# Seven block products for eight in the up-projection of the last 3072 tokens

## Chip, cores and metric

One core of a Trainium2 chip runs the whole program. The metric is the device time of one execution in microseconds (us). Engines are called as in the profile: PE (TensorE matmul), PEld (its weight loads), DVE (VectorE), ACT (ScalarE), POOL (GpSimd), SP (the queue that issues the DMAs).

## Reference

Attention over 8 batches, 8 heads, 576 positions and 64 channels, with a local mask in the first four heads and a strided one in the others; its output, as 4608 tokens by 512 channels, goes through a feed-forward layer.

```python
mask_local = (rel >= 0) & (rel < stride)                       # stride = 32
mask_strided = (rel >= 0) & (pos[None, :] % stride == pos[:, None] % stride)
...
attn = attn / (np.sum(attn, axis=-1, keepdims=True) + 1e-09)
attn_out = np.matmul(attn, v)
...
x = np.ascontiguousarray(attn_out.transpose(0, 2, 1, 3)).reshape(B * S, H * D)
h = np.maximum(x @ w_in, 0.0)                                  # 512 -> 2048
return (h * h @ w_out).astype(np.float32)                      # 2048 -> 512
```

## The kernel before

Tokens go in 12 chunks of 384 (`TC`). Every operand of the two big products is kept as a high and a low part of type fp32r, and a product is three matmuls: high by high, high by low, low by high.

**Feed-forward.** `up(c, j)` makes one of 16 tiles of 128 hidden units of chunk c: 4 slices of 128 channels by 3 parts, 12 matmuls of 384 columns (L440), in one of three PSUM banks. ACT takes relu and square of it in place (L451, L452) and casts the high part (L453); DVE subtracts to get the low part (L454). `down(c, j)` multiplies that tile into three output tiles: 3 times 3 matmuls of 512 columns (L473). PE takes two `up`, then the two `down` of the tiles before, so that ACT and DVE have the length of two `up` and two `down` for a tile. Chunk after chunk goes on without a break in this pattern.

**Attention** for a chunk is made while PE works on the chunk before it. `pair(c, pr)` does two local heads: 8 score matmuls (L219; the two heads sit in partitions 0 to 63 and 64 to 127, and alternate), masked minima on DVE (L222), 8 exps on ACT (L229), the division on ACT and POOL (L235, L237), 12 small transposes on DVE (L243), 8 output matmuls (L253). `strided(c)` does the other four heads on POOL and DVE alone: products on POOL (L390, L412), each summed by a DVE reduction (L391, L413). `plan` and `SPREAD` say at which tile of a chunk each step is issued. The weights are read once, split by ACT, DVE and POOL during the first chunk, and stay in SBUF.

**Order.** The scheduler fixes one order per engine ahead of time, and each engine keeps to it: an instruction whose data is late holds up all behind it on its engine.

## Time and profile before

| | before |
|---|---|
| median of 3 runs | 887.97 us (887.94 to 888.25) |
| the profiled execution: time | 888.65 us |
| the profiled execution: span | 886.9 us |
| PE busy | 877.0 us, 99% |
| DVE, ACT, POOL busy | 557.0, 444.0, 530.1 us |
| HBM read, written | 52.69 MB, 9.44 MB |

The span is from the first to the last instruction; 1.75 us lie around it. In the timeline a matmul's length holds its way through the array too, so lengths overlap: the time that a matmul takes from PE is the distance from its start to the next one's start.

### The profile page before, as it was taken

What the parts mean: (1) busy time and instruction counts of PE and PEld (TensorE: products, weight loads), DVE (VectorE), ACT (ScalarE), POOL (GpSimd) and SP (SyncE); (2) the same over time, 40 slices, a digit from 0 to 9 for tenths busy, and PEclk for the clock granted to TensorE, in tenths of its full rate; (3) what the DMA queues carried; (4) which work ended last, traced back from release to release, by engine and by line L of the source; (5) the groups of instructions that cost most, each with busy time, mean ns of one, the idle gap of its engine ahead of it and who ended that gap; (6) DMA issues with size and microseconds to landing.
All of it is one profiled execution on the core that took longest, in us unless ns stands there. A gap on an engine that the chain in (4) does not pass through costs nothing.

```text
span 886.9 us, 14492 instructions
## 1 busy us (share of the span) xinstructions
PE 877.0 (99%) x5107; PEld 783.0 (88%) x5107; DVE 557.0 (63%) x1640; ACT 444.0 (50%) x1166; POOL 530.1 (60%) x568
## 2 busy tenths in 40 slices
PE   8999999999999999999999999999999999999997
PEld 7788898989898988898889898989898889898996
DVE  5786677687677677777867868868777333241111
ACT  5999645355355353453544535435535445353332
POOL 3699666767857787887787788788878101000000
PEclk9999999999999999999999999999999999999999
DMA  9852511140031121120211212202101100000000
GB/s 361 334 210 94 186 57 52 62 143 25 18 131 32 66 100 31 57 78 17 76 46 49 64 39 67 64 13 82 58 13 55 31 13 35 14 1 2 35 1 36
DMA packets 21033, 63.06 MB, mean 71 GB/s; under 512 B 2336, under 2 KB 2976, under 8 KB 19424
## 3 DMA queue, kind: packets, MB, share of 16 engines
q1 hardware_dynamic: 20672, 61.81, 20.4%
q8 instruction: 40, 0.66, 0.3%
q10 hardware_dynamic: 288, 0.33, 0.1%
q14 instruction: 33, 0.27, 0.1%
HBM read 52.69 MB, written 9.44 MB: 70 GB/s over the span
## 4 chain that ended last, share of the span: by engine, by line
PE 95%; ACT 2%; POOL 1%; issue 0%; DVE 0%; DVEq 0%; POOLq 0%; ACTq 0%
PE h L440 45%; PE y L473 45%; PE s L219 2%; PE o L253 2%; ACT b L317 1%; PE w_ps L570 1%; PE b L289 1%; POOL w L171 1%; ACT raw L152 0%; ACT z L164 0%; POOL pq L390 0%; ACT w L170 0%; PE b L345 0%; ACT xsh L360 0%; PE b L333 0%
## 5 line engine op out<-in xcount | busy, mean ns | idle before, releaser
L473 PE MATMUL y<-w,gh 128*128 128x512 f32 x1152 | 356.9, 393 | 0.5 <-POOL w L171 0.5
L473 PEld LDWEIGHTS y<-w,gh 128*128 128x128 f32 x1152 | 213.6, 188 | 43.9 <-POOL w L171 0.8
L440 PE MATMUL h<-xlh,w 128*128 128x384 f32 x768 | 230.6, 341 | 1.3 <-ACT xlh L360 0.6
L412 POOL TENSOR_TENSOR pp<-vs,sc 128x448 f32<-128x448 f32 (+10 forms) x192 | 188.7, 1013 | 67.4 <-issue 38.9
L440 PE MATMUL h<-xsh,w 128*128 128x384 f32 x768 | 226.4, 335 | 0.3 <-POOL w L171 0.3
L473 PE MATMUL y<-w,gl 128*128 128x512 f32 x576 | 222.5, 392 | 0.0
L390 POOL TENSOR_TENSOR pq<-ks,qs 128x512 f32<-128x512 f32 (+2 forms) x192 | 196.6, 1050 | 36.0 <-DVE sc L391 29.3
L454 DVE TENSOR_TENSOR gl<-h,gh 128x384 fp32r<-128x384 f32 x192 | 105.8, 552 | 149.7 <-ACT gh L453 147.4
L451 ACT ACTIVATE h<-h 128x384 f32<-128x384 f32 x176 | 83.1, 472 | 205.9 <-PE h L440 205.8
L453 ACT CAST gh<-h 128x384 fp32r<-128x384 f32 x192 | 92.0, 479 | 175.7 <-PE y L473 170.2
L391 DVE TENSOR_REDUCE sc<-pq 128x8 f32<-128x512 f32 (+4 forms) x228 | 118.4, 535 | 64.3 <-POOL pq L390 61.9
L440 PEld LDWEIGHTS h<-xlh,w 128*128 128x128 f32 x768 | 141.2, 188 | 8.3 <-ACT w L170 0.9
L440 PEld LDWEIGHTS h<-xsh,w 128*128 128x128 f32 x768 | 141.3, 188 | 1.1 <-POOL w L171 0.6
L413 DVE TENSOR_REDUCE qs<-pp 128x64 f32<-128x448 f32 (+11 forms) x192 | 106.8, 564 | 38.1 <-POOL pp L412 35.8
L440 PE MATMUL h<-xll,w 128*128 128x384 f32 x384 | 129.1, 336 | 0.0
L440 PE MATMUL h<-xsl,w 128*128 128x384 f32 x384 | 128.4, 334 | 0.0
L473 PEld LDWEIGHTS y<-w,gl 128*128 128x128 f32 x576 | 108.1, 188 | 22.8
L452 ACT ACTIVATE h<-h 128x384 f32<-128x384 f32 x176 | 83.4, 475 | 4.6
L243 DVE STREAM_TRANSPOSE p_t<-e 32x128 f32<-32x128 f32 x240 | 71.8, 300 | 6.9 <-POOL e L237 2.5
L440 PEld LDWEIGHTS h<-xll,w 128*128 128x128 f32 x384 | 72.1, 188 | 3.2 <-DVE xll L361 0.3
L440 PEld LDWEIGHTS h<-xsl,w 128*128 128x128 f32 x384 | 72.1, 188 | 0.2
L229 ACT ACTIVATE e<-e,nm 96x128 f32<-96x128 f32 x160 | 62.1, 390 | 18.0 <-DVE nm L222 18.0
(88 smaller groups left out, 665.4 us busy)
## 6 DMA issues: line engine op xcount, KB each, us to landing
y<-ysb SPq DMA_DIRECT2D x36, 256.0 KB, 2.0
raw<-w_in SPq DMA_DIRECT2D x7, 1024.0 KB, 10.8
v<-v_d SPq DMA_DIRECT2D x24, 256.0 KB, 2.7
vs<-v_s SPq DMA_DIRECT2D x10, 576.0 KB, 3.8
raw<-w_out SPq DMA_DIRECT2D x5, 1024.0 KB, 12.5
qk<-qk_d SPq DMA_DIRECT2D x12, 416.0 KB, 3.5
qk<-qk_d SPq DMA_DIRECT2D x12, 400.0 KB, 3.1
ks<-k_s SPq DMA_DIRECT2D x8, 576.0 KB, 3.8
```

The source lines that it names most:

```text
L229: nc.scalar.activation(e4[h][:, w], e4[h][:, w], AF.Exp, bias=nm[:QC, h, w : w + 1], scale=-1.0, accum_out=ss[:QC, NW * h + w, :1])
L243: nc.vector.transpose(out=p_t[h][STR * k : STR * (k + 1), :, STR * r : STR * (r + 1)], in_=ev[STR * r : STR * (r + 1), :, STR * k : STR * ...
L390: nc.gpsimd.tensor_mul(pv, kt[:, a : a + m, :], qt[:, i - i0 : i - i0 + 1, :].broadcast_to([P, m, D]))
L391: nc.vector.tensor_reduce(out=sc[:, i - i0, a : a + m], in_=pv, op=ALU.add, axis=AX.X)
L412: nc.gpsimd.tensor_mul(pv, vt[:, a : a + nd, :n], sc[:, il : il + 1, :n].broadcast_to([P, nd, n]))
L413: nc.vector.tensor_reduce(out=ot[:, il, a : a + nd], in_=pv, op=ALU.add, axis=AX.X)
L440: done = nc.tensor.matmul(ph[:, :TC], w[:, wsl], xx, start=n == 0, stop=n == 11)
L451: nc.scalar.activation(g, g, AF.Relu)
L452: nc.scalar.activation(g, g, AF.Square)
L453: last["gh"] = nc.scalar.copy(gh, g)
L454: nc.vector.tensor_sub(gl, g, f32(gh))
L473: done = nc.tensor.matmul(y_ps[c][t], g[:, sl], w[:, wsl], start=j == 0 and k == 0, stop=j == NFT - 1 and k == 2)
```

## The change

Chunks 0 to 3 stay as they are. The last 3072 tokens (attention chunks 4 to 11) go in 6 blocks of 512 tokens, each in 8 steps (`q` counts them, 0 to 47) of 256 hidden units. A step's up-projection is a product of 2 by 2 blocks (128 hidden units by 256 channels, 256 channels by 256 tokens), made of 7 block products in place of 8 (`up7`). A block product is 6 matmuls of 256 columns (L702). Three PSUM banks, here x, y and a, take them: four times ACT copies what stands in a bank so far into SBUF (`keep`, L716), and product 4 goes into x on top of product 1, 5 into y on top of 2, 7 into x on top of 4. Three DVE additions (L730 to L732) make the two hidden tiles.

`combos` makes the weight sums on DVE and POOL during chunks 1 and 2, splits them into high and low on ACT and POOL, and writes all 7 per step to DRAM. `stream` reads the 7 (1.75 MB) for each step, two steps ahead, on SP's queue. `split_x` makes the 7 token operands of a block, and their parts, during the last step of the block before. `down7` is the down-projection of a step: 4 output tiles by 6 matmuls of 512 columns. Within a block PE takes `up7(q)`, then `down7(q-1)`; at a block's end `down7(q)` comes at once after `down7(q-1)`, and the next block begins with two `up7` in a row.

From chunk 6 on, `pair` puts its scores into banks 1 and 2 (y and a). `STARTS` and `PACE` replace `plan` and `SPREAD`: six pairs of chunks 2 to 4 stay within the old chunks, with both pairs of chunk 5; 12 pairs (chunks 6 to 11) fall into the blocks, at q = 0, 2, 8, 10, 14, 16, 18, 20, 22, 24, 30 and 32.

```diff
+STARTS = {
+    2: (8, 12), 3: (16, 20), 4: (22, 24), 5: (26, 28), 6: (32, 34),
+    7: (40, 42), 8: (46, 48), 9: (50, 52), 10: (54, 56), 11: (62, 64),
+}
...
-        s_ps = [psum(3 + h, f"s{h}{u}") for h in range(2)]
+        s_ps = [psum((3 + h) if c <= NCL + 1 else 1 + h, f"s{h}{u}") for h in range(2)]
...
+    def stream(q):
+        a = wpool.tile([P, 4, 2, 2 * P], F32R, name=f"ea{q}", tag=("w0", "w3")[q % 2])
+        b = wpool.tile([P, 3, 2, 2 * P], F32R, name=f"eb{q}", tag=("w1", "w5")[q % 2])
+        nc.sync.dma_start(out=f32(a), in_=scr[q % NPER][:, :4])
+        nc.sync.dma_start(out=f32(b), in_=scr[q % NPER][:, 4:])
...
+    def split_x(m):
...
+        split("1", b11, v)
+        v.tensor_sub(b11, b12, b11)
+        v.tensor_sub(b12, b22, b12)
+        split("7", b12, v)
+        split("2", b21, g)
+        split("3", b22, v)
+        v.tensor_sub(b22, b22, b11)
+        split("6", b22, v)
+        v.tensor_sub(b21, b21, b22)
+        split("4", b21, g)
+        split("5", b11, g)
...
+    def product(acc, e, x, start):
...
+            for kt in range(2):
+                wh, wl = (e[:, h, kt * P : (kt + 1) * P] for h in range(2))
+                for w, xx in ((wh, x[:, 0, kt]), (wh, x[:, 1, kt]), (wl, x[:, 0, kt])):
+                    done = nc.tensor.matmul(acc, w, xx, start=start and n == 0, stop=n == 5, skip_group_check=not start)
...
+    def up7(q):
...
+        product(x[:, :HS], e[0], opnd["1"], True)
+        keep(0, x)
+        product(y[:, :HS], e[1], opnd["7"], True)
+        keep(3, y)
+        product(a[:, :HS], e[2], opnd["2"], True)
+        product(x[:, :HS], e[3], opnd["6"], False)
+        keep(2, x)
+        product(y[:, :HS], e[4], opnd["4"], False)
+        product(a[:, HS:], e[5], opnd["3"], True)
+        product(x[:, :HS], e[6], opnd["5"], False)
+        keep(1, x)
+        with tc.high_priority():
+            nc.vector.tensor_add(h[1][:, :HS], y[:, :HS], vt[:, 2])
+            nc.vector.tensor_add(h[1][:, HS:], x[:, :HS], vt[:, 3])
+            nc.vector.tensor_add(h[0], a, vt[:, :2].rearrange("p a n -> p (a n)"))
...
+    def square(q, h):
...
+            nc.scalar.activation(h[o], h[o], AF.Relu)
+            nc.scalar.activation(h[o], h[o], AF.Square)
+            nc.scalar.copy(gh, h[o])
+            (nc.gpsimd if o else nc.vector).tensor_sub(gl, h[o], f32(gh))
...
+    for q in range(NM * NPER):
...
+        h = up7(q)
+        if q + 2 < NM * NPER:
+            stream(q + 2)
...
+        if p:
+            down7(q - 1, event)
+        else:
+            event()
+        square(q, h)
+        if p == NPER - 1:
+            if m + 1 < NM:
+                split_x(m + 1)
+        rest(k)
+        advance(NS + 2 * q + 1, {})
+        if p == NPER - 1:
+            down7(q)
```

Two places in the order of the built programs. First PE where a pair's scores stand (s0 and s1 are the two heads). Before, between the `up` and the `down` of a chunk:

```order
L219 MATMUL s03_0_2183<-qk3_0_2137 96x128
L219 MATMUL s13_0_2184<-qk3_0_2137 96x128
L219 MATMUL s03_0_2183<-qk3_0_2137 96x128
L219 MATMUL s13_0_2184<-qk3_0_2137 96x128
L219 MATMUL s03_0_2183<-qk3_0_2137 96x128
L219 MATMUL s13_0_2184<-qk3_0_2137 96x128
L219 MATMUL s03_0_2183<-qk3_0_2137 96x128
L219 MATMUL s13_0_2184<-qk3_0_2137 96x128
```

Now, at the start of the second block, where steps 8 and 9 follow each other (u0, u1, u2 are banks x, y, a):

```order
L702 MATMUL u2_8_5316<-op43_4152,eb8_5073 128x256 x6
L702 MATMUL u0_8_5314<-op5_4153,eb8_5073 128x256 x6
L265 MATMUL s07_0_5378<-qk7_0_5245 96x128 x4
L265 MATMUL s17_0_5379<-qk7_0_5245 96x128 x4
L702 MATMUL u0_9_5445<-op17_4150,ea9_5191 128x256 x6
L702 MATMUL u1_9_5446<-op17_4150,ea9_5191 128x256 x6
L702 MATMUL u2_9_5447<-op26_4151,ea9_5191 128x256 x6
L702 MATMUL u0_9_5445<-op26_4151,ea9_5191 128x256 x6
```

The heads no longer alternate: four of one, then four of the other. It is so for all 12 pairs from chunk 6 on; the eight of chunks 2 to 5 alternate as before.

Then ACT at the same place. Before, at the start of chunk 2 (h2_0 is the first tile, L453 its cast):

```order
L451 ACTIVATE h2_1_2160<-h2_1_2160 128x384
L452 ACTIVATE h2_1_2160<-h2_1_2160 128x384
L229 ACTIVATE e03_0_2179,sums0_94<-e03_0_2179,nm3_0_2181 96x128 x4
L229 ACTIVATE e13_0_2180,sums0_94<-e13_0_2180,nm3_0_2181 96x128 x4
L453 CAST gh2_0_2154<-h2_0_2141 128x384
```

Now, from the last copies of step 8 to those of step 9:

```order
L716 COPY ring_3198<-u0_8_5314 128x256 x2
L739 ACTIVATE h1_8_5318<-h1_8_5318 128x512
L739 ACTIVATE h0_8_5317<-h0_8_5317 128x512
L740 ACTIVATE h1_8_5318<-h1_8_5318 128x512
L275 ACTIVATE e07_0_5374,sums0_106<-e07_0_5374,nm7_0_5376 96x128 x3
L740 ACTIVATE h0_8_5317<-h0_8_5317 128x512
L275 ACTIVATE e07_0_5374,sums0_106<-e07_0_5374,nm7_0_5376 96x128
L741 CAST g_4154<-h1_8_5318 128x512
L716 COPY ring_3198<-u0_9_5445 128x256
L275 ACTIVATE e17_0_5375,sums0_106<-e17_0_5375,nm7_0_5376 96x128 x2
L716 COPY ring_3198<-u1_9_5446 128x256
L275 ACTIVATE e17_0_5375,sums0_106<-e17_0_5375,nm7_0_5376 96x128 x2
```

Behind these stand `L741 CAST` of h0_8, four divisions (L281), and the copy of u0_9 after product 4. Before, the one instruction of such a stretch that a later `up` waits for is the cast of h2_0 (it frees the bank for the third tile after it, which comes behind another `up` and two `down`); now three copies of step 9 stand among the exps and squares of step 8.

More of the change, by code (lines that the diff above doesn't have):

```diff
@@ L92, in attn_moe @@
     xpool = pool("xpool", 2)
+    dram = pool("dram", 1, space=bass.MemoryType.DRAM)
     gpool = pool("gpool", 2)
@@ L104, in psum @@
         return ps.tile([P, 512], F32, name=nm, tag=f"ps{i}")
+    spare = lpool.tile([P, 2304], F32, name="spare", tag="pt", bufs=1)
+    early = xpool.tile([P, 8 * TC], F32, name="early", tag="x")
+    scr = [dram.tile([P, 7, 2, 2 * P], F32, name=f"scr{p}") for p in range(NPER)]
     mask_sb = const.tile([P, 4, P], F32, name="mask_sb")
@@ L616, in attn_moe, with attention, advance @@
     zbank = (3, 4)
-    NS = NCHUNK * NFT
+    def attention():
+        for c in range(1, NCHUNK):
+            yield from strided(c)
+    st, lo, wc = attention(), behind(heads_end, local(1)), combos()
+    made = lo_made = 0
+    def advance(s, ins):
+        nonlocal made
+        gen = behind(ins, st)
+        while made < paced(s):
+            k = next(gen, None)
+            if k is None:
+                made = 1e9
+                return
+            made += k
+    NS = NCL * NFT
     for s in range(NS + 2):
         c, j = divmod(s, NFT)
+        k = s // 2
         if s < NFT:
@@ L630, in attn_moe @@
         elif s % 2 == 0:
-            before, between, rest = plan[j // 2]
-            for part, slots, two in (up, (s, s + 1), before), (down, (s - 2, s - 1), between):
-                take(c + 1, two)
+            if s < NS:
+                outputs(k)
+            for part, slots in (up, (s, s + 1)), (down, (s - 2, s - 1)):
+                if part is up and s >= NS:
+                    continue
                 with tc.issue_after(last["pe"].ins):
                     for i in slots:
-                        if 0 <= i < NS:
-                            last["mm"] = part(*divmod(i, NFT))
-                last["pe"] = last["mm"]
-            take(c + 1, rest)
+                        pe = part(*divmod(i, NFT))
+                last["pe"] = pe
+                if part is up and s < NS:
+                    scores(k)
+            if s < NS:
+                rest(k)
         if s < NFT - 2:
@@ L651, in attn_moe @@
                     nc.gpsimd.memset(t, 0.0)
[L652 to L674 removed]
+        if j == NFT - 2 and c == 0:
+            rest(NPER - 1)
@@ new lines, in attn_moe @@
+        if c == 0 and s >= LATER:
+            fl = (j + 1 - LATER) / 11
+            dl = round(fl * 10) if j < NFT - 1 else 10
+            while lo_made < min(dl, 10) and next(lo, "end") != "end":
+                lo_made += 1
+            advance(s, heads_end)
+        elif 0 < c < NCL:
+            advance(s, weights_end if c == 1 else {})
+            if c < 3:
+                gen = behind(weights_end if c == 1 else {}, wc)
+                next(gen, None)
+                next(gen, None)
+            if c == 2 and j == NFT - 1:
+                assert next(wc, None) is None
+                t = xpool.tile([P, 8 * TC], F32, name="ring", tag="x")
+                ring["l"] = t[:, : 2 * RING].rearrange("p (a n) -> p a n", a=2)
+                ring["v"] = t[:, 2 * RING :].rearrange("p (a n) -> p a n", a=4)
```

245 lines of the change are left out of this document (180 added, 65 removed).

## The prediction

> **What bounds the kernel now.** First the page's summary, the chain that ended last, and the costliest groups.
>
> ```profile
> PE 877.0 (99%) x5107; PEld 783.0 (88%) x5107; DVE 557.0 (63%) x1640; ACT 444.0 (50%) x1166; POOL 530.1 (60%) x568
> ...
> PE 95%; ACT 2%; POOL 1%; issue 0%; DVE 0%; DVEq 0%; POOLq 0%; ACTq 0%
> ...
> L473 PE MATMUL y<-w,gh 128*128 128x512 f32 x1152 | 356.9, 393 | 0.5 <-POOL w L171 0.5
> ...
> L440 PE MATMUL h<-xlh,w 128*128 128x384 f32 x768 | 230.6, 341 | 1.3 <-ACT xlh L360 0.6
> ```
>
> PE is never idle for long, and 95% of the chain is its own. Lengths overlap (393 ns for 512 columns), so the price of a matmul has to come from start to start. Second, windows of one chunk's length in the middle: they show whether anything but PE's own work sets the pace, and what the others have left.
>
> ```profile
> 393.00:463.10 70.10, 70.10 (x399) 62.72 (x398) 51.76 (x139) 32.37 (x89) 54.97 (x55) 1.00 0.17 53
> ...
> sum 210.30, PE 210.30 PEld 188.20 DVE 156.02 ACT 98.31 POOL 165.18; mean PE 70.10 PEld 62.73 DVE 52.01 ACT 32.77 POOL 55.06
> ```
>
> The columns after the window's length are PE, PEld, DVE, ACT, POOL, the granted clock (1.00), DMA share and GB/s. PE is busy for all of it, POOL for 79%, DVE for 74%. Third, PE's timeline for an `up`, a pair's scores and two `down`:
>
> ```profile
> 459.07 0.33 PE L440 MATMUL h<-xlh,w 128*128 128x384 f32 x1
> ...
> 460.98 0.34 PE L440 MATMUL h<-xsh,w 128*128 128x384 f32 x1
> 461.24 1.12 PE L219 MATMUL s<-qk 64*96 64x128 f32 x16
> 462.29 0.73 PE L473 MATMUL y<-w,gh 128*128 128x512 f32 x2
> 462.86 0.39 PE L473 MATMUL y<-w,gl 128*128 128x512 f32 x1
> ...
> 466.26 0.39 PE L473 MATMUL y<-w,gl 128*128 128x512 f32 x1
> ```
>
> The first and twelfth matmul of the `up` start 1.91 us apart: 11 steps of 0.1736. From 462.86 to 466.26 are 15 matmuls of 512 columns: 0.2267 each. A chunk by these is 8 x (24 x 0.1736 + 18 x 0.2267) = 66.0 us; 4.1 for two pairs of attention heads makes the 70.1 measured. The kernel is a row of matmuls laid end to end: what shortens the row counts, and so does each new gap in it.
>
> **The products: -23.7 us.** No row has 256 columns. The two rows above differ by 0.0531 for 128 columns, so 256 cost 0.1736 - 0.0531 = **0.1205**, if the fixed part (some 13 ns) stays. Below it the bound is the weight load:
>
> ```profile
> 26.89 0.19 PEld L440 LDWEIGHTS h<-xlh,w 128*128 128x128 f32 x1
> 27.00 0.19 PEld L440 LDWEIGHTS h<-xll,w 128*128 128x128 f32 x1
> ```
>
> After an idle stretch the second load starts 0.11 behind the first, so a load takes 0.11 before the next can begin, and a matmul can't take less. Above it the far bound is the load's recorded 0.188, were none of it hidden; but loads of 0.188 already follow each other every 0.1736, so I stay with 0.1205, with 0.110 and 0.130 for the range. For 512 tokens and 256 hidden units, before: 24 x 4/3 x 0.1736 = 5.555; now 42 x 0.1205 = 5.061. Saved: 0.494 x 48 steps = 23.7 us (0.110: 44.9; 0.130: 4.6; equal at 0.1323). The `down` matmuls stay 24 of 512 columns per 512 tokens.
>
> Two rules of the Trainium skill touch this price, both in "TensorE: Matmul & The Clock Gate". Part 3, "The mechanism", says that weight loads overlap matmuls in flight "only when row_grp differs"; all loads here use all rows, so each product matmul would cost 0.11 + 0.1205, 42 of them 9.7 us, and the change would lose 48 x 4.1 = 197 us. The timeline speaks against it: with the same rows and 384 columns the step is 0.1736, not 0.28. Part 1, "Wait — 56ns, not 53.3ns?", gives N / 2.4 GHz + 2.5 ns: 109 ns at 256 columns, and a saving of 47 us. It also gives 162.5 ns for 384 columns, where the rows have 173.6, so I don't lower the price.
>
> **The scores: +6.0 us.** A pair's 16 score matmuls (each of the 8 runs as two) cost PE 462.29 - 461.15 = 1.14. The heads alternate, in different rows of the array. From chunk 6 on they don't. What that does is seen in small matmuls of 96 columns early in the program, where two places in the array alternate (L356), or all use the same (L333):
>
> ```profile
> 16.13 0.88 PE L333 MATMUL b<-ident,e 96*128 96x96 f32 x8
> ...
> 23.20 1.51 PE L356 MATMUL b<-pt,v 96*32 96x96 f32 x32
> ```
>
> Less 0.25 for the last one's length: 1.26 / 31 = 0.041 each when alternating, 0.63 / 7 = 0.09 when not. So the run of 16, 0.85 without its last length, doubles: +0.85. Bounds: 0, and 1.0 if the switch of rows is paid twice. Of 12 such pairs 5 stand at a block's start, where the next term covers them; 7 x 0.85 = 6.0.
>
> **The block starts: +18.5 us.** At q = 0, 8, 16, 24 and 32, `up7(q)` and `up7(q+1)` stand back to back with a pair's scores between. Product 4 of step q+1 waits for the copy of product 1, product 5 for that of product 2, product 7 for that of product 4; ACT gives these copies the places that its order shows. Its prices:
>
> ```profile
> 494.30 0.40 ACT L229 ACTIVATE e<-e,nm 96x128 f32<-96x128 f32 x1 [1.37 <-DVE nm L222]
> ...
> 497.02 0.39 ACT L229 ACTIVATE e<-e,nm 96x128 f32<-96x128 f32 x1
> ...
> 497.40 0.47 ACT L451 ACTIVATE h<-h 128x384 f32<-128x384 f32 x1
> 497.81 1.26 ACT L235 ACTIVATE e<-e,rs 96x128 f32<-96x128 f32 x4
> 498.98 0.47 ACT L452 ACTIVATE h<-h 128x384 f32<-128x384 f32 x1
> ```
>
> Start to start: an exp 2.72 / 7 = 0.39, a division 1.17 / 4 = 0.29, 384 columns 0.41. A pass over 512 columns is 0.41 + 0.11 = 0.52 (the length grows by 0.1, from 0.47 to the 0.57 of L477), one over 256 columns 0.30:
>
> ```profile
> L454 DVE TENSOR_TENSOR gl<-h,gh 128x384 fp32r<-128x384 f32 x192 | 105.8, 552 | 149.7 <-ACT gh L453 147.4
> ...
> L477 ACT COPY ysb<-y 128x512 f32<-128x512 f32 x12 | 6.9, 573 | 4.7 <-PE y L473 4.7
> ```
>
> A DVE addition of 256 columns is about 0.42 and one of 512 about 0.68, on either side of the 0.552 for 384. With time 0 at the end of step 8's products: last copy 0.2 to 0.6, first hidden tile ready at 0.65, second at 1.35. ACT: relu 0.65, relu 1.35, square 1.9, three exps 2.4, square 3.55, exp 4.1, cast 4.45, and only then the copy of product 1 of step 9, 5.0 to 5.4. PE has done scores and products 1 to 3 by 2.0 + 2.2 = 4.2: it waits 1.2. Two exps, copy (to 6.5): product 5 waits 0.35 more. Two exps, cast, four divisions, copy (to 9.2): product 7 waits 1.3. Step 9 ends at 9.95; with scores as before and no wait 1.14 + 5.06 = 6.2. Lost: **3.7**, five times 18.5. The other orders (16, 24, 32: an output copy ahead of the relus) come out within 0.4 of it. Bounds per place: 0 (copies in time), and 6 if DVE's minima come 2 us late.
>
> At the seven other pairs `down7` lies between: the same ACT work takes until 9.2, product 4 of the next step comes at 10.5. Nothing is lost there, and 1 us of lateness is covered.
>
> **Small gaps: +3.7.** At q = 40 there is no pair, but bank x is free only 0.7 after the step. At the five block ends `down7` of the last step comes 5.4 after its products; its second hidden tile's low part is ready at 6.0 to 6.2 by the same prices (with two or three casts of `split_x` ahead on ACT), where PE's third matmul wants it at 5.9: 0.3 to 1, taken as 0.6. Bounds 0 and 2 each.
>
> **Work beside PE: +2.** Blocks 0 to 3 hold about 6 chunks' strided attention in 36 steps, 1.31 chunks each. By the windows' means POOL has 55.06 x 1.31 = 72, and per block 11 subtractions of 1.32 (the 512-column form of L171 below): 87 us. DVE has 52.0 - 10.2 (low parts, output copies) = 41.8 x 1.31 = 55, and 8 x 2.2 (two additions of 0.42, one of 0.68, a low part) + 7 (`split_x`, output) = 25: 80. ACT has 32.8 less 48 passes of 0.475, times 1.31, 13, and 8 x 4.3 + 5: 52. PE's own time for such a block is 8 x (5.06 + 5.44) + 9 for attention + 4 = 97. So POOL is at 90%, DVE at 82%, above the 79% and 74% of before, and not the bound. I take 2 us for lateness; bounds 0 and 20.
>
> ```profile
> L171 POOL TENSOR_TENSOR w<-raw,w 128x512 fp32r<-128x512 f32 x32 | 41.9, 1323 | 8.3 <-ACT w L170 8.3
> ```
>
> ```profile
> raw<-w_out SPq DMA_DIRECT2D x2, 1024.0 KB, 4.7
> ```
>
> At nothing I cost: `combos` (some 4 us on POOL and 2 on DVE per step's weights, in chunks 1 and 2, where both have 15 us per chunk to spare); the pairs that move into chunks 2 and 3 (PE does them either way); and `stream`. Around 50 us, with little else moving, 1 MB landed in 4.7 us, so 1.75 MB need some 8; from the release of its buffer to its use lie 15 or more. On SP a load of `vs` that waits for POOL can stand ahead of a stream, which leaves 7 us for POOL's lateness. If that cover is gone, each late stream costs its lateness.
>
> **Sum.** 888.65 - 23.7 + 6.0 + 18.5 + 3.7 + 2 = 895.2 for a profiled execution; it was 0.68 above the median of the three runs, so **894.5**. Likeliest: the change works as meant on PE and gives back more at its block starts and in its scores.
>
> **Rivals.**
> 1. *ACT's copies don't hold PE.* Faster. Place: product 4 of steps 1, 9, 17, 25, 33. If exps and squares are already done when step q+1's first product ends, the 18.5 vanish: 876. It decides below 2.4 us lost per place, where the sum is 888. For: before, ACT is idle half the time. Against: the fixed order and the prices above.
> 2. *A 256-column matmul takes the weight load's 0.11.* The sum falls by another 21 to 873. For: the load's spacing. Against: both larger sizes carry some 13 ns over their columns.
> 3. *POOL and DVE become the bound in blocks 0 to 3.* Each of POOL's multiplications waits for a DVE reduction, and the low parts stand between them in both queues. At 90% need it takes little: 4 to 5 us per block put the sum at 912. For: POOL's 87 of 97. Against: at 79% they cost PE nothing.
> 4. *Streams come late*, 48 times up to 1 us: 915 and more. Against: 15 us for 8.
>
> **Chances.** The forecast 0.50, with 886 to 905 as its own range, which holds most of what is the same (0.09); rival 1 0.24; rival 2 0.06; rival 3 0.17; rival 4 0.03; full loads by the first rule above under 0.01, its 197 us outside every range. 874 to 912 leaves out about 0.1 on each side. About 0.2% (1.8 us) is what a measurement of this kernel can tell from no change: faster 0.30, same 0.09, slower 0.61.
>
> **What the profile after would show.** Right: 256-column matmuls 0.12 apart; score rows x16 some 1.9 long from chunk 6 on; L702 waiting for the L716 copies, 3 us and more at five places; blocks of some 97 us, and of 84 to 86 when attention is done. Wrong: steps of 0.11 or 0.13 (the first term); no wait of L702 for L716 (rival 1); waits of `down7` for POOL's or DVE's low parts all over the first four blocks (rival 3); L702 waiting for DMA (rival 4).

## The result and the profile after

| | before | after |
|---|---|---|
| median | 887.96 us (887.47 to 888.25, 4 runs) | 950.82 us (949.36 to 951.93, 4 runs) |
| the profiled execution: time, span | 888.65, 886.9 us | 950.65, 948.8 us |

The change makes the kernel slower: the ratio is 1.0708, with a 95% interval of 1.0689 to 1.0726. The forecast was 894.5, its range 874 to 912. The sign was right, the size was not. First the summary and the chain of the changed kernel:

```profile
PE 883.6 (93%) x5587; PEld 776.5 (82%) x5587; DVE 682.9 (72%) x1776; ACT 518.5 (55%) x1334; POOL 661.8 (70%) x664
...
PE 44%; DVE 21%; POOL 16%; ACT 11%; issue 5%; DMA 3%; ACTq 0%; POOLq 0%; DVEq 0%
```

PE held 95% of the chain before, now 44%. What it waits for, by the view of its waits (sum in us, times, longest):

```profile
PE yy L758 <- ACT g L741: 21.8, 5, 6.8
PE yy L758 <- DVE g L742: 10.2, 6, 3.2
PE u L702 <- ACT ring L716: 9.8, 13, 1.5
PE h L499 <- DVE gl L513: 6.8, 4, 2.4
```

The 32 us in front of L758 (`down7`) come in 11 waits. All but 0.5 us of them stand at the ends of blocks, where `split_x` makes the next block's operands. One such end, the step q = 7, in the timelines of PE, ACT, DVE and POOL (start, length, what; in brackets the idle time ahead and who ended it):

```profile
418.27 3.04 PE L702 MATMUL u<-op,ea 128*128 128x256 f32 x24
...
423.30 5.63 PE L758 MATMUL yy<-w,g 128*128 128x512 f32 x24
433.11 1.22 PE L758 MATMUL yy<-w,g 128*128 128x512 f32 x2 [4.17 <-ACT g L741]
435.04 0.79 PE L758 MATMUL yy<-w,g 128*128 128x512 f32 x1 [0.71 <-DVE g L742]
435.63 1.48 PE L758 MATMUL yy<-w,op 128*128 128x512 f32 x3
...
440.87 0.84 PE L758 MATMUL yy<-w,g 128*128 128x512 f32 x3
...
442.23 3.04 PE L702 MATMUL u<-op,ea 128*128 128x256 f32 x24
```

```profile
428.80 0.62 ACT L675 CAST op<-spare 128x512 fp32r<-128x512 f32 x1 [2.86 <-DVE spare L684]
429.32 1.14 ACT L739 ACTIVATE h<-h 128x512 f32<-128x512 f32 x2
...
432.44 0.61 ACT L741 CAST g<-h 128x512 fp32r<-128x512 f32 x1
```

```profile
424.41 0.41 DVE L730 TENSOR_TENSOR h<-u,ring 128x256 f32<-128x256 f32 x1
424.75 1.45 DVE L676 TENSOR_TENSOR op<-spare,op 128x512 fp32r<-128x512 f32 x1
426.12 0.94 DVE L676 TENSOR_TENSOR op<-ring,op 128x512 fp32r<-128x512 f32 x1
426.99 1.77 DVE L684 TENSOR_TENSOR spare<-spare,ring 128x512 f32<-128x512 f32 x1
428.69 0.41 DVE L731 TENSOR_TENSOR h<-u,ring 128x256 f32<-128x256 f32 x1
429.02 0.68 DVE L732 TENSOR_TENSOR h<-u,ring 128x512 f32<-128x512 f32 x1
```

```profile
423.90 2.61 POOL L440 TENSOR_TENSOR pq<-ks,qs 128x512 f32<-128x512 f32 x2
426.48 1.74 POOL L676 TENSOR_TENSOR op<-ring,op 128x512 fp32r<-128x512 f32 x1
```

PE is done with the step's products at 423.3. On DVE the additions that make the hidden tiles (L731, L732) stand behind three operations of `split_x`, and start at 428.7 only. On ACT the relus (L739) stand behind a cast that waits for the last of the three. So the hidden tiles' high parts come at 433, and PE has idled for 4.2 us and then 0.7. Behind this gap three matmuls take 1.48 in place of 0.84: the array runs at about half its rate (0.43 for 0.227 per matmul) for some 4 us. From q = 7 to the next block are 23.96 us; 5.04 of products and two `down7` of 5.44 make 15.9.

The ends at q = 15, 23 and 31 are alike but for two things: the small transposes of a pair (L289) stand ahead of the additions too, and the relus start 8.1, 7.1 and 6.4 us after the products, 2.3, 0.9 and 0.8 us after the cast ahead of them has ended. So there it is DVE's addition that they wait for last, not ACT's cast; at q = 15:

```profile
531.85 0.62 ACT L675 CAST op<-ring 128x512 fp32r<-128x512 f32 x1 [4.57 <-DVE ring L679]
534.78 1.17 ACT L739 ACTIVATE h<-h 128x512 f32<-128x512 f32 x2 [2.31 <-DVE h L731]
```

At q = 7 DVE's three operations take 1.45, 0.94 and 1.77, where L732, over as many columns, takes 0.68. L732 reads one operand from PSUM; the three read both from SBUF. L684 ends (428.76) 0.54 after POOL's L676 has ended (428.22). The groups of whole kernels, kept apart by shape, show the same:

```profile
L742 DVE TENSOR_TENSOR g<-h,g 128x512 fp32r<-128x512 f32 x48 | 55.9, 1165 | 36.6 <-ACT g L741 36.3
...
L732 DVE TENSOR_TENSOR h<-u,ring 128x512 f32<-128x512 f32 x48 | 32.7, 680 | 0.0
...
L730 DVE TENSOR_TENSOR h<-u,ring 128x256 f32<-128x256 f32 x48 | 20.2, 421 | 36.6 <-PE u L702 36.0
...
L636 DVE TENSOR_TENSOR spare<-spare 128x256 f32<-128x256 f32 x8 | 8.4, 1055 | 2.2 <-POOL spare L631 2.2
```

Before, no large DVE operation had both operands in SBUF (L454 reads the hidden tile from PSUM). A small one had, L397 of the strided attention, and its rows in the profile of before show the same: 36 columns took 0.20 where POOL was idle, and 1.98 where POOL's L171, which reads SBUF, ran four times in a row:

```profile
46.81 1.98 DVE L397 TENSOR_TENSOR sc<-sc,mx 128x36 f32<-128x36 f32 x1
...
110.62 0.20 DVE L397 TENSOR_TENSOR sc<-sc,mx 128x36 f32<-128x36 f32 x1
```

### The profile page after: what moved, and what is told of

Same layout as the page of the kernel before. It is cut to its first block, busy times and chain, and to the rows that moved or that the text cites. A ratio compares the mean times of both kernels' runs of the same rounds, so it can differ in the third digit from the quotient of the medians.

```text
span 948.8 us, 16167 instructions
## 1 busy us (share of the span) xinstructions
PE 883.6 (93%) x5587; PEld 776.5 (82%) x5587; DVE 682.9 (72%) x1776; ACT 518.5 (55%) x1334; POOL 661.8 (70%) x664
## 4 chain that ended last, share of the span: by engine, by line
PE 44%; DVE 21%; POOL 16%; ACT 11%; issue 5%; DMA 3%; ACTq 0%; POOLq 0%; DVEq 0%
PE yy L758 19%; PE u L702 17%; POOL pp L462 5%; POOL pq L440 5%; DVE p_t L289 4%; PE y L532 3%; DVE op L676 3%; DVE sc L441 2%; PE h L499 2%; ACT e L275 2%; DMA scr<-so 2%; POOL w L209 2%; DVE qs L463 1%; POOL so L644 1%; ACT h L739 1%
## 5 line engine op out<-in xcount | busy, mean ns | idle before, releaser
L758 PE MATMUL yy<-w,g 128*128 128x512 f32 x864 | 226.5, 402 | 32.0 <-ACT g L741 21.8
L462 POOL TENSOR_TENSOR pp<-vs,sc 128x448 f32<-128x448 f32 (+10 forms) x192 | 197.3, 1054 | 47.5 <-DVE qs L463 24.5
L758 PEld LDWEIGHTS yy<-w,g 128*128 128x128 f32 x864 | 162.1, 193 | 70.5 <-ACT g L741 24.0
L499 PE MATMUL h<-x,w 128*128 128x384 f32 x768 | 148.1, 343 | 11.7 <-DVE gl L513 6.8
L702 PE MATMUL u<-op,ea 128*128 128x256 f32 x1152 | 150.3, 285 | 6.9 <-ACT ring L716 5.0
L702 PEld LDWEIGHTS u<-op,ea 128*128 128x128 f32 x1152 | 144.8, 191 | 14.5 <-ACT ring L716 7.5
L716 ACT COPY ring<-u 128x256 f32<-128x256 f32 x192 | 70.5, 371 | 153.5 <-PE u L702 152.1
L499 PEld LDWEIGHTS h<-x,w 128*128 128x128 f32 x768 | 135.2, 190 | 19.3 <-DVE gl L513 10.7
L532 PE MATMUL y<-w,gh 128*128 128x512 f32 x384 | 119.8, 396 | 0.5 <-POOL w L209 0.5
L702 PE MATMUL u<-op,eb 128*128 128x256 f32 x864 | 113.5, 284 | 5.1 <-ACT ring L716 4.7
L702 PEld LDWEIGHTS u<-op,eb 128*128 128x128 f32 x864 | 107.3, 192 | 7.3 <-ACT ring L716 7.3
L739 ACT ACTIVATE h<-h 128x512 f32<-128x512 f32 x96 | 58.9, 632 | 62.8 <-DVE h L731 62.3
L758 PE MATMUL yy<-w,op 128*128 128x512 f32 x288 | 86.0, 409 | 0.0
L532 PEld LDWEIGHTS y<-w,gh 128*128 128x128 f32 x384 | 71.8, 189 | 15.3 <-POOL w L209 0.8
L742 DVE TENSOR_TENSOR g<-h,g 128x512 fp32r<-128x512 f32 x48 | 55.9, 1165 | 36.6 <-ACT g L741 36.3
L742 POOL TENSOR_TENSOR g<-h,g 128x512 fp32r<-128x512 f32 x24 | 32.1, 1339 | 63.1 <-ACT g L741 63.0
L289 DVE STREAM_TRANSPOSE p_t<-e 32x128 f32<-32x128 f32 x240 | 72.1, 300 | 3.9 <-ACT e L281 1.0
L742 POOL TENSOR_TENSOR op<-h,op 128x512 fp32r<-128x512 f32 x24 | 36.3, 1513 | 55.2 <-ACT op L741 49.3
L532 PE MATMUL y<-w,gl 128*128 128x512 f32 x192 | 73.4, 394 | 0.0
## 6 DMA issues: line engine op xcount, KB each, us to landing
raw<-w_in SPq DMA_DIRECT2D x7, 1024.0 KB, 11.2
```

Source lines behind the costliest of these rows:

```text
L289: nc.vector.transpose(out=p_t[h][STR * k : STR * (k + 1), :, STR * r : STR * (r + 1)], in_=ev[STR * r : STR * (r + 1), :, STR * k : STR * ...
L462: nc.gpsimd.tensor_mul(pv, vt[:, a : a + nd, :n], sc[:, il : il + 1, :n].broadcast_to([P, nd, n]))
L499: done = nc.tensor.matmul(ph[:, :TC], w[:, wsl], xx, start=n == 0, stop=n == 11)
L532: done = nc.tensor.matmul(y_ps[c][t], g[:, sl], w[:, wsl], start=j == 0 and k == 0, stop=j == NFT - 1 and k == 2)
L702: done = nc.tensor.matmul(acc, w, xx, start=start and n == 0, stop=n == 5, skip_group_check=not start)
L716: nc.scalar.copy(vt[:, i], src[:, :HS])
```

## The ledger

In us, after against before; the starts of steps are those of their first L702 in PE's timeline.

| term | predicted | measured |
|---|---|---|
| products | -23.7 | -24.7: 256 columns every 0.120, so 42 in 5.04; 48 x (5.555 - 5.04) |
| scores of the seven pairs inside blocks | +6.0 | +5.5: from first score to next matmul 12.9, at 1.05 before 7.4 |
| block starts 0 to 4: second `up7` and the scores ahead of it | +18.5 | +19.6: 7.5 to 8.0 from first to last matmul where 4.92 is free of waits, 13.9; five runs of scores 10.9, at 1.05 before 5.3 |
| third and fourth `up7` of blocks 0 to 3 | 0 | +3.7: 5.1 to 6.5 at six places where 4.92 is free of waits |
| q = 40 | +0.7 | +1.1 |
| block ends, q = 7, 15, 23, 31, 39 | +3.0 | +45.8: 24.0, 29.3, 27.9, 26.5 and 17.7, each less 15.9 |
| `combos` in chunks 1 and 2 | 0 | +15.6: from chunk 1 to q = 0 238.4; before 214.6 to chunk 4, and 8.2 for two pairs and 18 matmuls that are ahead of q = 0 now |
| beside PE | +2 | in the terms above |

The terms measured make 66.6, 4.6 more than the 62.0 by which the profiled executions differ. An error in the account of before works the other way: a chunk there took 70.9 from start to start (chunks 4 and 5 begin at 315.15 and 386.06), and the 70.1 that the prediction called measured was the length of its window, not a distance between chunks. These 0.8 us, for 8 chunks 6.4, were saved too and stand in no term; 1.8 us stay unexplained. Half of the 6.4 is PE's own work: two `up` and two `down` in a chunk without attention took 8.31, for 512 tokens 11.08, and a step of block 5 takes 10.50, so that 48 steps save 27.8 and not 24.7. Of the 45.8 at the block ends some 34 are waits, and some 8 are matmuls at the lower clock behind them. So two terms failed, block ends and `combos`; the experiments are on these first.

## Experiments: the block ends

Kernels are edits of the changed kernel, if nothing else is said.

**split_behind.**

```diff
-        square(q, h)
+        ends = square(q, h)
...
+                with ExitStack() as st2:
+                    for i in ends:
+                        st2.enter_context(tc.issue_after(i.ins))
                     split_x(m + 1)
```

> Only the order is changed: split_x of the next block is put behind the squares of step 7 of a block on ACT, DVE and POOL. Theory A (order): at the four ends of blocks 0 to 3 the relus of step 7 stand on ACT behind casts of split_x (L675) that wait for DVE's subtractions, so PE waits in the last down7 for L741 and L742 (32 us in all, and a lower clock behind each gap). Then the stretch from the first product of q = 7, 15, 23, 31 to that of the next block falls from 24, 29, 28 and 26 us to some 16 to 20, and the time from 950.8 to 920 to 932. Theory B (too much work on DVE and POOL): the wait only changes its place, to the first products of the next block that need the operands; the time stays between 943 and 955.

933.64 us, ratio to before 1.0514 (1.0499 to 1.0530), between the ranges of the two theories. The ends fall to 16.4, 18.0, 18.3 and 19.0, as theory A has it, but the first two steps of a block grow, together from 84 to 105 us in blocks 1 to 4, as B has it: PE now waits for operands there. So order is a good part of it; the rest came back as waits for what `split_x` makes.

**adds_first.** The edit names only DVE's order; in the built program the casts of `split_x` that wait for DVE's sums come behind the relus as well.

```diff
-            nc.vector.tensor_add(h[0], a, vt[:, :2].rearrange("p a n -> p (a n)"))
+            last["h0"] = nc.vector.tensor_add(h[0], a, vt[:, :2].rearrange("p a n -> p (a n)"))
...
+        with tc.issue_after(last["h0"].ins) if m else ExitStack():
             split("1", b11, v)
...
```

> Only DVE's order is changed at the ends of blocks: split_x's sums and low parts are queued behind the three additions that make the hidden tiles of step 7. Theory A (DVE's queue: each operation of split_x on two SBUF operands waits for a multiplication on POOL, and the additions stand behind them, so ACT gets the hidden tiles 5 us late): the ends of blocks 0 to 3 fall from 24 to 29 us to 15 to 19, as with split_x behind all of the squares, and the time to 925 to 936, with longer first steps of the next block. Theory B (ACT's casts in front of the relus are what holds): ends stay above 22, the time above 942.

926.32 us, 1.0431 (1.0413 to 1.0448); 24.5 below the changed kernel, in A's range. Ends of 17.6, 21.4, 20.3 and 22.9: below the changed kernel's, but only the first in A's range, and the fourth in B's. DVE and ACT at q = 7 in its timeline (products end at 422.5):

```profile
423.14 0.42 DVE L732 TENSOR_TENSOR h<-u,ring 128x256 f32<-128x256 f32 x1 [1.31 <-ACT ring L717]
423.49 0.68 DVE L733 TENSOR_TENSOR h<-u,ring 128x512 f32<-128x512 f32 x1
```

```profile
423.60 1.29 ACT L740 ACTIVATE h<-h 128x512 f32<-128x512 f32 x2 [0.49 <-DVE h L732]
...
426.35 0.62 ACT L742 CAST g<-h 128x512 fp32r<-128x512 f32 x1
```

The relus start 1 us after the products, where they started 6 after; at the other three ends 3.2, 2.3 and 3.4 after. No other edit of order alone gives back more (even, below, 22.9).

**early_sums.** Three sums of token blocks move one step ahead, and the casts stand right behind the products.

```diff
+        v.tensor_sub(t5, b12, b11)
+        v.tensor_sub(b12, b22, b12)
+        v.tensor_sub(t6, b22, t5)
...
         h = up7(q)
+        if p == NPER - 1 and m + 1 < NM:
+            split_x(m + 1)
```

> Three of the four sums of token blocks for the next block (split_x) are made one step earlier, into two tiles that are free in the blocks, and the casts and low parts are written right behind the products of step 7, so no cast on ACT stands ahead of the relus waiting for a sum on DVE. Theory A (the order: a cast that waits for DVE's sums holds the relus): the ends of blocks 0 to 3 fall from 24 to 29 us to 13 to 17, without the longer first steps that the kernel with split_x behind the squares showed, and the time falls to 908 to 925. Theory B (work and locks on DVE and POOL): ends stay above 20, the time above 938.

955.25 us, 1.0749 (1.0729 to 1.0769): theory A missed, with ends of 25.2, 24.5, 30.0 and 27.1. The trace shows why: ACT's casts were early (at q = 23 and 31 all that stand ahead of the relus end 1.1 us after the products), but their low parts (DVE) now stood ahead of the additions. At q = 23 the relus wait for an addition, L738, alone:

```profile
645.34 0.62 ACT L683 CAST op<-t 128x512 fp32r<-128x512 f32 x1
654.27 1.17 ACT L746 ACTIVATE h<-h 128x512 f32<-128x512 f32 x2 [8.30 <-DVE h L738]
```

With ACT's casts out of the way these ends are no shorter; this parts DVE's order from ACT's, which adds_first alone doesn't.

**lows_dve.** Both low parts of a step on DVE.

```diff
-            (nc.gpsimd if o else nc.vector).tensor_sub(gl, h[o], f32(gh))
+            nc.vector.tensor_sub(gl, h[o], f32(gh))
```

> Both low parts of a step (L742) are made on DVE, none on POOL; nothing else is changed. Theory A (exclusion): DVE's low parts now wait only for the strided multiplications, their mean falls from 1.165 to below 1.0 us, POOL has 11 us less per block, and the time falls by 4 to 15, to 936 to 947. Theory B (DVE is the fuller engine at the block ends, and everything waits in its queue): the second low part adds to DVE's queue, ends grow from 24 to 29 us to 26 to 32, and the time is 952 to 965.

955.26 us, 1.0752 (1.0734 to 1.0770). The mean fell to 0.986, as A says; the time did not, and lies in B's range. But the ends are 26.6, 26.6, 29.1 and 24.7, together as long as in the changed kernel, so that B's reason, longer ends, isn't shown. Of its 96 low parts, 49 took 0.65 to 0.69; each of the other 47, up to 1.79 long, ended 0.55 after an operation of POOL, most often a multiplication of the strided attention.

**pool_fill.**

```diff
-                    nc.gpsimd.tensor_mul(pv, kt[:, a : a + m, :], qt[:, i - i0 : i - i0 + 1, :].broadcast_to([P, m, D]))
+                    for _ in range(FILLS):
+                        nc.gpsimd.memset(pv, 1e-3)
...
```

`FILLS` is 2, and the second multiplication (L462) is replaced in the same way.

> POOL's multiplications of the strided attention are replaced by two fills of the same region, so POOL writes as often but reads nothing there; the strided heads' results are left out by this. Theory A (a DVE operation with both operands in SBUF and a POOL operation that reads SBUF exclude each other): L742 on DVE falls from a mean of 1.165 us to 0.70, L676 and L684 on DVE from 1.1 to 1.6 to 0.70, while L732 (one operand in PSUM) stays at 0.68; the time falls to 915 to 930. Theory B (DVE's operations on two SBUF operands are slow by themselves): L742 stays above 1.1, and the time falls only by what POOL's shorter queue gives, to 938 to 948.

921.03 us, 1.0377 (1.0360 to 1.0395). The time is A's; the mean of L742 (here L745) is not, it stays at 1.191, because POOL's own low part of the same step is a reader too: 35 of the 48 begin beside it. `split_x`'s operations on DVE, L676 and L684 (here L679 and L687), fall from 1.36 and 1.33 to 0.79 and 0.75. Two places in the timeline tell the two neighbours apart:

```profile
358.34 1.28 POOL L745 TENSOR_TENSOR op<-h,op 128x512 fp32r<-128x512 f32 x1
358.44 1.73 DVE L745 TENSOR_TENSOR g<-h,g 128x512 fp32r<-128x512 f32 x1
...
509.54 0.82 POOL L442 MEMSET pq<- 128x512 f32 x3
509.59 0.69 DVE L745 TENSOR_TENSOR g<-h,g 128x512 fp32r<-128x512 f32 x1
```

Beside a low part on POOL, DVE's takes 1.73 and ends 0.55 after it; beside fills, which read nothing, 0.69. So it is not slow by itself. The run also shortens POOL's queue (two fills of 512 columns take 0.99, a multiplication 1.29), and what of the 30 us comes from that and what from the exclusion isn't shown.

**even.**

```diff
-        if p:
+        if q:
             down7(q - 1, event)
...
-        if p == NPER - 1:
-            down7(q)
+    down7(NM * NPER - 1)
```

> Only the order on PE at a block's edge is changed: down7(q-1) stands behind up7(q) at every q, so the last down7 of a block follows the first up7 of the next, and no two up7 stand back to back. Theory A (the back-to-back places wait for ACT's copies and squares, some 3 us at five places, and the last down7 comes before its hidden tiles are ready): the steps behind a block's start lose their 7.5 us forms (5.0 instead), and the time falls to 915 to 930, with what is left as waits of the first up7 of a block for its operands. Theory B (split_x and the low parts are late as a whole): the same time is waited for in front of the next block's first products, and the time stays above 940.

927.89 us, 1.0450 (1.0435 to 1.0466), in A's range. The second `up7` of blocks 1 to 4 is nearly free of waits (5.8 at most, where 4.92 is free); but the first one now takes 11.6 to 13.6, since its operands come late. A part of what the edges cost has moved, as B says, and 23 us are gone.

## Experiments: the weight sums and the scores

In chunk 2 of the changed kernel a cast of a sum (L643) stands on ACT for 3.53 us until the one buffer is written to DRAM, with a relu behind it; DVE's low part is late two tiles on, and PE waits:

```profile
222.46 0.41 ACT L643 CAST so<-spare 128x256 fp32r<-128x256 f32 x1 [3.53 <-DMA scr<-so]
222.77 0.47 ACT L510 ACTIVATE h<-h 128x384 f32<-128x384 f32 x1
```

```profile
225.17 2.27 PE L499 MATMUL h<-x,w 128*128 128x384 f32 x12
229.80 2.98 PE L499 MATMUL h<-x,w 128*128 128x384 f32 x12 [2.36 <-DVE gl L513]
```

**no_sums, so_wide, sums_behind.** No sums at all; three of four staging tiles in columns that are free by then; casts and additions queued behind the hidden tiles' own.

```diff
-            full = spare[:, :1024]
...
+            for i in (1, 3, 5, 6):
+                nc.sync.dma_start(out=scr[p][:, i], in_=f32(pieces[p][:, :, : 2 * P]))
...
```

```diff
+DEAD = {1: 0, 3: 512, 6: 1280}
...
-                so = lpool.tile([P, 2, 2 * P], F32R, name=f"so{p}_{i}", tag="so", bufs=1)
...
+                    so = spare[:, DEAD[i] : DEAD[i] + 4 * P].bitcast(F32R).rearrange("p (a n) -> p a n", a=2)
```

```diff
-                gen = behind(weights_end if c == 1 else {}, wc)
+                gen = behind((weights_end if c == 1 else {}) | {"gh": last["gh"], "gl": last["gl"]}, wc)
```

> The sums of weight blocks are left out (plain weight blocks are written to DRAM in their places), so four of seven products have wrong weights. This prices everything that combos does on ACT, DVE and POOL. My prediction put it at nothing (chunks 1 to 3 stay at 238); by the comparison of the two traces it is 15.6 us: chunks 1 to 3 in 222 to 225 us and the time 934 to 937.

> Three of the four staging tiles of each set of sums take dead columns of spare instead of the one buffer so. Theory A (ACT's casts L643 stand in its queue waiting for the write of the buffer before them to DRAM, 28.8 us of idle ACT, with the relus of the products behind them): chunks 1 to 3 take 238.4 us now and fall to 226 to 231, the time to 938 to 944. Theory B (the additions themselves on DVE and POOL make the low parts late): chunks 1 to 3 stay above 235, the time above 946.

> Only the place of the weight sums in chunks 1 and 2 is changed: their casts are queued on ACT behind the casts of the hidden tiles made in the same pair of steps, and their additions on DVE behind the low parts. Theory A (ACT's cast of a sum stands ahead of the relus and waits for DVE or for the buffer's write to DRAM): chunks 1 to 3 fall from 238.4 to 226 to 231 us, the time to 939 to 945. Theory B (the work of the sums on DVE and POOL, with the waits between these two engines, is what costs): chunks 1 to 3 stay above 235 and the time above 946.

no_sums: 942.13 us, 1.0608 (1.0592 to 1.0624). From chunk 1 to q = 0 it takes 223.3, as expected; but the last weights are converted later in its order and chunk 1 begins 12 us late, so that the time shows 8.7 only. so_wide: 945.08, 1.0643 (1.0627 to 1.0659), the stretch 236.3. sums_behind: 947.37, 1.0666 (1.0650 to 1.0682), 235.4. Both stretches miss theory A's and lie where B puts them, each 2 to 3 us better than in the changed kernel; the time of so_wide lies between the two theories. With both edits (six_four, below) the stretch is 233.1. So the sums cost 15, of which place and staging give back 5. That the other 10 go with the work itself is argued, not shown: DVE and POOL are 77 to 82% busy in chunks 1 and 2, and 71 to 79% without the sums.

**alt_scores.** Each score matmul behind the one before it (`tc.issue_after(last["mm"].ins)`).

> Only the order of the 16 score matmuls of a pair is changed: each is queued behind the one before it, so the two heads alternate again. My prediction's second term says that a run of 16 falls from some 1.95 to 1.14 us, 12 times: the time falls by 6 to 10, to 941 to 946. Rival: the scores lie in stretches in which PE waits anyway (a block's first steps wait for ACT's copies), and the time stays between 948 and 952.

945.40 us, 1.0642 (1.0624 to 1.0660): 5.4 less, at the edge of the range. The order is as meant, but the 12 runs still take 21.0 from first score to next matmul, against 23.8 and, before, 12.6; so 2.8 of the 5.4 lie in them. Six of them wait in the middle for bank 2, which L732 (DVE) releases, and take 13.0 where 6.3 is free of waits. In the changed kernel a run without a wait takes 1.56, 0.51 more than before: 6.1 of the 11.2 for 12 runs; the other 5.1 are waits. So order and bank each cost about a half there, and with the order mended the bank, wanted earlier in a run, takes a part of it back.

## Experiments: together, and in fewer blocks

**all_four** is even, early_sums, alt_scores and so_wide, with `tc.high_priority()` around the relus, casts and low parts of chunks 1 to 3. **six_four** is adds_first, alt_scores, so_wide and sums_behind.

> The three edits of this call together, the wider staging of the weight sums, and a higher priority for the relus, casts and low parts of chunks 1 to 3. PE's own work from the first up7 on is 48 x 10.48 us, 12 pairs of some 2.1, and 3 at the end: 531 us; before it 26 + 74 + 223 = 323 without a wait. If order and the edges of blocks are what the change lost (theory A): 862 to 888, below the kernel before. If DVE's and POOL's work and their exclusion of each other is the bound in blocks 0 to 3 (theory B): blocks of 97 us and more, and a time above 900.

> Four edits together on the changed kernel: the additions ahead of split_x on DVE (alone -24.5), alternating scores (-5.4), wider staging of the sums (-5.7), and the sums queued behind (not known). If the causes are separate they add up: 905 to 915. If they share one bound (DVE and POOL have no time left in blocks 0 to 3), the sum is not reached: 918 to 926.

all_four: 921.96 us, 1.0377 (1.0360 to 1.0393): B's time, though only blocks 1 and 2 of the first four are as long as B says (100 and 104 us; 0 and 3 take 94 and 92). six_four: 919.85, 1.0362 (1.0327 to 1.0396), 31 below the changed kernel where the edits alone gave 24.5, 5.4, 5.7 and 3.5: 39. Of the 8 that are missing, 6.4 stand at one place: the first step of block 4 takes 14.1 for 7.75, since PE waits there for operands that `split_x` makes on DVE and POOL. It fits the shared bound of the expectation. DVE and POOL are busy for most of blocks 0 to 3:

```profile
338.40:442.20 103.80, 94.86 (x593) 82.47 (x592) 82.04 (x184) 52.19 (x134) 85.31 (x79) 0.97 0.55 193
...
859.40:948.00 88.60, 84.54 (x529) 76.13 (x527) 24.18 (x34) 39.80 (x83) 10.29 (x8) 1.00 0.41 143
```

These are the windows of blocks 0 and 5 of the changed kernel (columns as in the prediction). In block 5 attention is done. Block 0's 85 us of POOL and 82 of DVE are close to the 87 and 80 that the prediction has for a block; it put them in 97 us, and the block took 104.

**three_plain, three_blocks, three_tuned, three_spread, three_paused.** The seven products for the last 1536 tokens only.

```diff
-NCL = 4
+NCL = 8
...
-        for c in range(1, NCHUNK):
+        for c in (1, 2, 3, 4, 8, 5, 6, 7, 9, 10, 11):
             yield from strided(c)
...
```

`STARTS` and `PACE` are moved to match. three_blocks adds even, early_sums, adds_first, alt_scores and so_wide; three_tuned adds sums_behind and makes the first split two steps earlier; three_spread and three_paused alter three_tuned's pace, as their expectations say, and spread the sums:

```diff
-            if c < 3:
+            if c < 5 and s % 4 < 3:
                 gen = behind((weights_end if c == 1 else {}) | {"gh": last["gh"], "gl": last["gl"]}, wc)
```

> The seven products only for the last 1536 tokens, in 3 blocks for 6 (NCL = 8, with the plan of pairs and the pace of the strided attention moved accordingly and the sums spread over 43 steps), edges as in the changed kernel. By the theory that the loss lies at the edges of blocks in which DVE and POOL still have attention, at two ends of 10 and three starts of 3, and in the sums (some 10): 895 to 908. By a rival, that the loss goes with the tokens (each step a little too long): half of 62, 919.

> The same 3 blocks, with down7(q-1) behind up7(q) at every q, alternating scores, sums of token blocks one step earlier and their later low parts behind the additions of the hidden tiles, and the wider staging of the weight sums. PE's own work by the traces so far: 599 to the first up7, 24 x 10.5, two pairs more before and two in the blocks at 2.1 each, 4 for the last down and 3.5 at the end: 871. With 5 to 12 us of waits for the sums and the edges: 876 to 884, below the kernel before. If POOL and DVE hold the blocks again: 890 and more.

> Three blocks (the last 1536 tokens) with all the edits on order, the sums queued behind the hidden tiles, and the first split of tokens made two steps earlier. The kernel three_blocks took 900.9 with 11 us lost in chunk 1 and 7 in front of its first block's second product; if both go, 882 to 889, at or just below the kernel before. If the sums cost the same wherever they are queued, 893 and more.

> three_tuned with three edits: the weight sums in three of four steps over 43 steps for 32, the strided attention some 2% earlier, and the first split of tokens in three parts over three steps for two parts. Theory A (what is left are these waits): chunk 2 from 75.0 to 73 us, chunk 5 from 72.9 to 71, chunk 7 from 82.1 to 78, so 882 to 888, at or just below the kernel before. Theory B (the work of sums and splits on DVE and POOL costs wherever it stands): 890 to 894.

> three_tuned with the sums spread over 43 steps and with the strided attention's pace held still in the last five half-steps of chunk 7 and in the last two steps of the first block, a little faster elsewhere. If the split's operations are late because they queue among the strided attention's (theory A), chunk 7 takes 78 us and the first block stays at 86: 884 to 889, equal to the kernel before or just below it. If the split itself is too long for its place (theory B): 890 to 896.

| kernel | median, us | ratio to before, 95% interval |
|---|---|---|
| three_plain | 903.81 | 1.0178 (1.0163 to 1.0194) |
| three_blocks | 900.91 | 1.0139 (1.0124 to 1.0155) |
| three_tuned | 892.50 | 1.0049 (1.0034 to 1.0064) |
| three_spread | 896.54 | 1.0101 (1.0084 to 1.0117) |
| three_paused | 892.72 | 1.0051 (1.0037 to 1.0066) |

three_plain, with a half of the tokens, loses 16 of 63 us: the loss doesn't go with the tokens. That is in its range, in part by luck: its two ends lose 6.9 and 1.8 where 10 each were expected, and the chunks ahead some 14 where 10 were. three_blocks lies where its rival has it, at 890 and more; three_tuned between its two theories, three_spread above both, three_paused where theory B has it. In three_tuned PE hardly waits in the blocks; the windows of its three:

```profile
621.00:707.00 86.00, 84.75 (x570) 75.42 (x569) 70.77 (x170) 49.65 (x131) 70.02 (x65) 1.00 0.58 204
707.00:798.00 91.00, 89.78 (x595) 79.64 (x594) 56.95 (x138) 53.27 (x135) 42.38 (x39) 1.00 0.50 177
798.00:890.00 92.00, 89.72 (x552) 80.39 (x550) 26.01 (x37) 40.40 (x84) 11.96 (x9) 1.00 0.40 142
```

PE is busy for 98% of them at full clock. But the eight chunks ahead lose some 14 us to sums, to attention made earlier and to the first split. three_spread and three_paused moved these waits (a wait of 2.7 us for a low part in chunk 7 stayed in the second) and didn't remove them. No version was found that beats the kernel before; whether one exists is open.

## Why the prediction was wrong, point by point

- **What bounds the kernel:** right. PE had no gap to lose, and each new gap came out in the time.
- **Products, -23.7:** right, by mechanism and size (0.120 us against 0.1205). Both rules of the Trainium skill that the prediction weighed against the rows, on weight loads and on N / 2.4 GHz ("TensorE: Matmul & The Clock Gate", Part 3, "The mechanism", and Part 1, "Wait — 56ns, not 53.3ns?"), give other numbers than the 0.120 measured here: 0.23 and 0.109.
- **Scores, +6.0:** +5.5, in part by luck. Without a wait a run took 1.56 for 1.05, so 0.51 for the 0.85 taken; what was overlooked is that the second head's bank is one that L732 has to release first, and waits for it in two of the seven runs made up the rest.
- **Block starts, +18.5:** right, 19.6: 13.9 in the products, where 2.85 at each of five places was forecast, and 5.7 in the scores ahead of them. The waits stand for L716, as forecast; the longest is 1.5. In the steps behind them (2, 10, 11, 18, 19 and 27) `up7` lost another 3.7, for which there was no term.
- **Small gaps, +3.7:** here the prediction failed, in the five block ends, taken as 0.6 each with bounds of 0 and 2; they cost 45.8. It followed ACT's order, with "two or three casts of `split_x` ahead", and took DVE's additions as ready at once after the products. In DVE's order three operations of `split_x` stand ahead of them (adds_first, which puts them behind: -24.5), and they took 0.7 to 3.2 each for the 0.68 assumed, 0.9 to 1.8 at q = 7. And it had no term for the clock: behind waits of 4 us and more the array took 0.43 for 0.227 per matmul, some 8 of the 45.8.
- **The price of a DVE operation** was taken from L454, which reads PSUM. No large row of before has both operands in SBUF, and the small one that has, L397, shows what was missing: 36 columns took 0.20 alone and 1.98 beside POOL. From it the price should have had a POOL operation's 1.3 on top as a bound. The Trainium skill has the rule that speaks against the change here ("SBUF — State Buffer", "Who interferes with whom"): a DVE instruction with two SBUF inputs and a GpSimd instruction that reads SBUF exclude each other, the second one waits until the first has ended. The prediction didn't weigh it; the trace agrees (1.73 beside a reading POOL operation, 0.69 beside a fill).
- **Work beside PE, +2 (bounds 0 and 20), and `combos` at nothing:** the second was wrong by 15.6, and this step failed too. "15 us per chunk to spare" is a mean over a chunk; PE wants a tile within two `up` and two `down`, 8.3 us, and waits for low parts (L513) that come later. The place of the sums in the queues and their one buffer are 5 of the 15; how the rest arises stays open.
- **Rivals:** 1, 2 and 4 did not come (L702 waited for L716; no matmul took 0.11; streams were not waited for). Rival 3 had the place nearly right, DVE and POOL in blocks 0 to 3, and 912 for it; but the waits were not "all over the first four blocks", they stood at their ends.

## What to carry to other kernels

Price an operation by a row with its operands in the same memories: a DVE operation that reads SBUF twice is not the one that reads PSUM once, once POOL works beside it. Where a rare step (here once in 8) is put on engines that are 80% busy, read their order at that step, for every engine on the way to PE, and not their mean load. A saving of a few per cent on the bounding engine, paid for with work on its helpers, is worth what the edges leave of it: in three blocks with all edges in order the seven products still cost 0.5%.

## What the runs showed of the hardware

DVE with two operands in SBUF and POOL reading SBUF excluded each other: DVE's low parts of 512 columns took 0.65 to 0.69 us, or ended 0.55 after an operation of POOL (39 of 48 in the changed kernel, 47 of 96 in lows_dve, 35 of 48 in pool_fill). The other way round, 15 of POOL's low parts in the changed kernel began while such an operation ran on DVE and took 1.74 in the middle, the other 33 took 1.29. The array's clock fell behind gaps: 0.43 for 0.227 per matmul of 512 columns for some 4 us behind 4.2 us of idling, and even behind the 2.36 us in chunk 2 (12 matmuls in 2.98 for 2.27). The granted clock there (the column ahead of the DMA share; PE's busy time comes first):

```profile
227.90:231.29 3.39, 1.49 (x8) 1.49 (x9) 3.35 (x11) 3.17 (x13) 3.18 (x3) 1.00 0.21 77
231.29:234.70 3.41, 3.41 (x10) 2.95 (x10) 3.32 (x7) 1.86 (x5) 3.41 (x4) 0.50 0.00 0
234.70:238.10 3.40, 3.40 (x22) 2.58 (x22) 3.30 (x9) 0.88 (x3) 1.68 (x4) 1.00 0.20 77
```

It halved 1.5 us after the wait had ended, for 3.41 us. Waits of 1.62 and 1.94 us in the same chunk had no such stretch behind them. The Trainium skill ("TensorE: Matmul & The Clock Gate", Part 1, "What's actually happening") gives half clock after an idle window of about 3.4 us; the 4.2 us agree, the 2.36 us were shorter than that.
